# Attention and MLP in one layer: each step's scores from one half of the array's rows, and eight products with v in a row on the other half

## The chip, the cores and the metric

One core of a Trainium2 chip. The metric is the device time of one execution in microseconds; the median of the runs is compared. A profile is one further execution with the hardware profiler, and its times are used for the analysis.

## The reference

```python
xn = layernorm(x)                                   # x: 1 x 2048 x 512, float32
qkv = xn @ wqkv; q, k, v = split in 32 heads of 16
p = softmax(einsum("bhqd,bhkd->bhqk", q, k) * 16 ** -0.5)
A = einsum("bhqk,bhkd->bhqd", p, v).merge_heads() @ wo
B = gelu(xn @ w1 + b1) @ w2 + b2                    # hidden size 1792
out = x + A + B
```

All inputs are float32. The kernel splits the operands of most products into two float16 parts (high and low), and three products of parts stand for one.

## The kernel before

**Tiling.** The 32 heads are eight groups of four; the 2048 queries are four blocks of 512. Group and block give 32 blocks of work, and each has 16 units; a unit is a step of `unit` (512 steps in all). Everything on TensorE (PE) in the main part uses one half of the array's rows (a *side*: rows 0 to 63 or 64 to 127) and a quarter of its columns per instruction; `tiled` (L195) issues four instructions, one per quarter, and this is called a *group of four* or, for short, a product. Two heads lie on each side: heads 0 and 2 on side 0, 1 and 3 on side 1.

**A step** (`unit`, L581) makes, for each of the four heads:

- `s_half` (L238): a score tile with queries as rows into a bank S (three banks), and on VectorE (DVE) the maximum along it (L250). These serve the *later* step: after 16 steps the block's maxima are negated (L261), transposed and turned into two float16 rows (`store`, L264: PE, DVE, GpSimd, then DMAs to `m_d` and from there into two spare rows of the query tile `qst`).
- `e_half` (L286), LEAD = 20 steps behind `s_half`: a score tile with keys as rows into a bank T (three banks); the two spare rows subtract the maximum; ScalarE (ACT) writes the exponential (L297) into a tile `pe`, of which there are 12.
- `v_half` (L300): the float32 products of the four heads' `pe` with v on one side, accumulated over the whole block in one bank V. The array's quarters hold the four heads. A block's sums need both sides of each unit, so V is written by both sides in turn.

A step has two halves. In each the order on PE is: score for the maximum, score for the exponential, twice, alternating between the sides; then `v_half` on one side (r = 1 in the first half, for the unit two steps back, r = 0 in the second, one step back); then `dense` products on the other side.

**Dense work** comes from a generator in `Group`s: the projections of q and k for later heads (24 groups, 12 products a side), then the MLP for four blocks of 512 tokens (14 hidden groups of 12, then 4 groups of 42), then the output projection. How many are issued in a half step is the group's `pace`: FAST four, SLOW three, MEAN three and four in turn (L32). Hidden groups alternate SLOW and FAST (L980), the second matmul is SLOW in the first two blocks and MEAN after (L1000). A group's accumulator is a bank D or T; both sides write it. At its end ACT, DVE (`hh`, L976) or GpSimd work follows.

**Turns.** Two sides must not write one bank at the same time. Before each half step `enter` (L187) sets a goal, and the first v or dense product waits (L173) on one semaphore, `turns`, until the last v and the last dense product of the half before are complete (`leave`, L178). This wait stands in PE's queue, so all that is behind it waits as well.

**Other queues.** The order on every compute engine is the order in which the program issues. GpSimd's work is dosed in `run_steps` (L219) to 2500 ns per step, and things are put off by steps with `later`. All DMAs are issued by SyncE (SP), in order.

**The weight of the output projection**, `wo_s` (L94), is split into two float16 parts in the preparation (L898) and stays in on-chip memory to the end; `wo_l` is a copy of some of its rows on other partitions (L1059). After the MLP its pool is given up, and the pool of the output projection takes the space (L1056).

Of the kernel before, what the change touches and what calls it, by code (L numbers as in the profile page):

```python
# [33 lines left out]
HALF = 1300  # L34
# [13 lines left out]
def layer_kernel(ctx: ExitStack, tc: tile.TileContext, x, wqkv, wo, w1, b1, w2, b2, out):  # L48
# [17 lines left out]
    w2_d = dram.tile([P, 2, NF, D], F16, name="w2_d")  # L66
    acc_d = dram.tile([S, D], F32, name="acc_d")
# [26 lines left out]
    wo_s = const.tile([P, 2, NC, D], F16, name="wo_s")  # L94
# [53 lines left out]
    def split_pool(hi, lo, src, inv):  # L148
        nc.scalar.activation(hi, src, AF.Copy, scale=inv)
        given("act", 1000)  # L150
        nc.gpsimd.tensor_scalar(src, src, inv, 0.0, op0=ALU.mult, op1=ALU.add)
        nc.gpsimd.tensor_tensor(lo, src, hi, op=ALU.subtract)
# [4 lines left out]
    backlog = {"act": 0, "dve": 0}  # L157

    def given(engine, ns):
        backlog[engine] += ns  # L160

    turns = tc.alloc_semaphore("turns")
    counted, left, newest, goal = [0], [], {}, [None]

    def product(user, *args, **kw):

        p = nc.tensor.matmul(*args, **kw)  # L169
        if user is None:  # L170
            return
        if goal[0] is not None:
            p._wait_ge(turns, counted[0])  # L173
            tc.declare_fence(p.ins, group=goal[0])
            goal[0] = None
        newest[user] = p

    def leave(user, goes_on):  # L178

        p = newest.pop(user, None)  # L180
        if p is not None and goes_on:
            p.then_inc(turns, 1)
            tc.no_tile_sem_insts.add(p.ins.name)
            counted[0] += 1
            left.append(p)

    def enter():  # L187

        if left:
            goal[0] = f"turn{counted[0]}"  # L190
            for p in left:
                tc.add_to_no_dep_group(goal[0], p.ins)
            left.clear()

    def tiled(user, dst, lhs, rhs, start, stop):  # L195

        for j in range(0, P, 32):
            product(user, dst[j:j + 32], lhs[:, j:j + 32], rhs, start=start, stop=stop)


    mt_of, ptiles, pv_of = {}, {}, {}
# [36 lines left out]
    def s_half(u, n):  # L238
# [10 lines left out]
        tiled(None, s, qs[p][qb][r, qt * P:(qt + 1) * P], ks[p][kb][r, :], True, True)  # L249
        nc.vector.reduce_max(mt_of[t][:, n, qt, kb:kb + 1], s, axis=AX.X)  # L250
        given("dve", 600)

    def s_end(u):
# [8 lines left out]
        given("dve", 220)  # L262

        def store():  # L264
# [7 lines left out]
            given("dve", 220)  # L272
# [13 lines left out]
    def e_half(u, n):  # L286
# [7 lines left out]
        tiled(None, st, kst[g % 2][p][kt // 4][r, k0:k0 + P], qst[g % 2][p][qb][r, :], True, True)  # L294
        pe = work.tile([P, QB], F32, name="pe", bufs=12)
        ptiles[u, n] = pe
        nc.scalar.activation(pe, st, AF.Exp, scale=sexp[:, g // 2:g // 2 + 1])  # L297
        given("act", 580)

    def v_half(u, a):  # L300

        t, kt = divmod(u, 16)
        g, qb = divmod(t, NQB)
        if kt == 0 and a == 0:
            pv_of[t] = hold("V", "S")
        pv = pv_of[t][0]
        r = slice(64 * a, 64 * a + 64)
        for h in (2, 3, 0, 1):
            c = (4 * g + h) * VW
            product("V", pv[32 * h:32 * h + 32, :], vv[r, kt, c:c + 32], ptiles[u, h][r],  # L310
                    start=(kt == 0 and a == 0), stop=(kt == 15 and a == 1))

    def v_end(u):

        t, kt = divmod(u, 16)
        g, qb = divmod(t, NQB)
        for h in range(4):
            del ptiles[u, h]
        if kt < 15:
            return  # L320
# [3 lines left out]
        given("act", 600)  # L324
# [12 lines left out]
        def inverse():  # L337
            nc.vector.reciprocal(dn, dn)
            given("dve", 330)
# [64 lines left out]
    class Group:  # L404
# [15 lines left out]
        def product(self, side):  # L420
# [11 lines left out]
            tiled("D", self.bank, lhs[r], rhs[r], start, self.last and self.over())  # L432
# [43 lines left out]
    def project(m, w, sb, wh, bank, early=False):  # L476
# [6 lines left out]
        def finish(pj):  # L483
# [5 lines left out]
            given("act", 600)  # L489
# [51 lines left out]
    def ended():  # L541

        if cur[0] is not None and cur[0].over():
            done, cur[0] = cur[0], None
            done.end()
# [10 lines left out]
    def dense(gen, side):  # L556

        f = group(gen)
        for _ in range(0 if f is None else f.pace[pos[0] % 2]):
            if not f.usable(side):  # L560
                return
            f.product(side)

# [9 lines left out]
    def unit(gen):  # L573


        u = pos[0]
        e = u - LEAD
        if u == LEAD and cur[0] is not None:
            burst(gen, cur[0].left())
        pos[0] += 1  # L580
        for a in range(2):  # L581
            for b in range(2 * a, 2 * a + 2):
                if u < NU:
                    s_half(u, b)
                if 0 <= e < NU:
                    e_half(e, b ^ 1)
            if e >= 0:
                enter()

                w, r = (e - 2, 1) if a == 0 else (e - 1, 0)  # L590
                live = 0 <= w < NU
                new = r == 0 and w % 16 == 0
                if live and not new:
                    v_half(w, r)
                dense(gen, 1 - r)
                if live and new:
                    v_half(w, r)

                for user, goes_on in (("V", live and not (r == 1 and w % 16 == 15)),
                                      ("D", cur[0] is not None and not cur[0].over())):  # L600
                    leave(user, goes_on)
# [525 lines left out]
```

## Time and profile before

| | us |
|---|---|
| median of 3 runs | 1575.26 (1571.25 to 1576.23) |
| the profiled execution, device time | 1573.2 |
| its span, first to last instruction | 1571.4 |
| PE busy | 1514.5 |
| DVE busy | 1418.4 |
| ACT busy | 1368.2 |
| GpSimd busy | 668.9 |

The granted TensorE clock is 0.991 of full speed in the mean. A matmul's span in the profile has a modelled end, and neighbours overlap, so busy shares of PE, DVE and ACT run somewhat high; the distance between starts is the better measure. PEld is the loading of weights. A chain of waits is followed back from the last instruction; each piece is the work, or the transfer, that ended last.

### The profile page before, as it was taken

The page shows a single profiled execution, that of the slowest core. Times are in us where ns is not written, and L with a number is a line of the kernel's source. Part 1 is how long each engine was busy: PE and PEld are TensorE (multiplying, and loading weights), DVE is VectorE, ACT ScalarE, POOL GpSimd, SP SyncE. Part 2 cuts the span into 40 slices and gives each one's busy share as a digit, 9 for nine tenths or more (in the row PEclk, how much of TensorE's full clock was granted, in tenths as well). Part 3 has the DMA queues.
Part 4 walks back from the last instruction along what each step waited for, and adds up shares of the span by engine and source line. Part 5 has one row for each costly group of instructions (what it writes and reads, how often), then busy time and mean ns, then how long its engine had stood idle before and what let it go on. Part 6 is the DMA issues. An engine that isn't in the chain of part 4 may idle for free.

```text
span 1571.4 us, 85965 instructions
## 1 busy us (share of the span) xinstructions
PE 1514.5 (96%) x38915; PEld 813.5 (52%) x38915; DVE 1418.4 (90%) x2388; ACT 1368.2 (87%) x2254; POOL 668.9 (43%) x742
## 2 busy tenths in 40 slices
PE   8997998999999999999999999999999999999998
PEld 3433554545555555555455555555555555555443
DVE  7896997989999999999899999999999999999911
ACT  4314998989999999999899999999999999999893
POOL 3113586717774211667511147781116775211000
PEclk9998999999999999999999999999999999999999
DMA  6466366361112111121111111221112110102323
GB/s 205 131 209 219 110 173 209 120 197 48 47 46 67 41 34 38 55 57 45 54 36 51 34 51 44 58 72 33 34 47 59 42 35 15 38 26 86 97 86 102
DMA packets 120248, 123.71 MB, mean 79 GB/s; under 512 B 38988, under 2 KB 90572, under 8 KB 119880
## 3 DMA queue, kind: packets, MB, share of 16 engines
q1 hardware_dynamic: 119880, 118.21, 25.0%
q8 instruction: 304, 4.98, 1.3%
q14 instruction: 64, 0.52, 0.1%
HBM read 80.61 MB, written 37.34 MB: 75 GB/s over the span
## 4 chain that ended last, share of the span: by engine, by line
PE 67%; DVE 20%; DMA 5%; POOL 3%; issue 2%; SPq 1%; ACT 1%; DVEq 0%; POOLq 0%
PE pV L169 20%; DVE mt L250 16%; PE pD L169 15%; PE pS L169 14%; PE pT L169 13%; DVE hh L976 2%; DMA wch<-in_B_w_dram 1%; PE pD L428 1%; DMA m_d<-mhl 1%; PE pT L428 1%; DVE amx L637 1%; SPq L355 1%; PE pT L521 1%; DMA qst<-m_d 1%; PE pS L428 0%
## 5 line engine op out<-in xcount | busy, mean ns | idle before, releaser
L297 ACT ACTIVATE pe<-pT,sexp 128x512 f32<-128x512 f32 x2048 | 1266.7, 689 | 81.3 <-PE pT L169 34.5
L250 DVE TENSOR_REDUCE mt<-pS 128x1 f32<-128x512 f32 x2048 | 1289.2, 683 | 47.5 <-PE pS L169 29.2
L169 PE MATMUL pV<-pe,vv 64*32 64x512 f32 x8192 | 1078.8, 597 | 1.1 <-PE pS L169 0.7
L169 PE MATMUL pT<-qst,kst 64*32 64x512 f16 x8192 | 708.2, 379 | 11.0 <-DMA qst<-m_d 7.8
L169 PE MATMUL pS<-kst,qst 62*32 62x512 f16 x8192 | 637.9, 380 | 30.1 <-DVE mt L250 25.4
L169 PEld LDWEIGHTS <-qst 62*32 62x32 f16 x8192 | 279.8, 92 | 269.0 <-issue 131.1
L169 PEld LDWEIGHTS <-kst 64*32 64x32 f16 x8192 | 295.1, 91 | 183.4 <-issue 68.5
L169 PE MATMUL pD<-xb,wc 64*32 64x512 f16 x5376 | 363.2, 378 | 2.5 <-DMA kst<-qk_d 2.5
L169 PE MATMUL pD<-w_s,g 64*32 64x512 f16 x5376 | 365.4, 377 | 0.0
L169 PEld LDWEIGHTS pV<-pe,vv 64*32 64x32 f32 x8192 | 181.7, 105 | 96.3 <-PE pS L169 7.6
L169 PEld LDWEIGHTS <-wc 64*32 64x32 f16 x5376 | 121.0, 92 | 55.9 <-issue 6.3
L169 PEld LDWEIGHTS <-g 64*32 64x32 f16 x5376 | 112.1, 91 | 44.7 <-issue 0.4
L169 PE MATMUL pD<-xt,wqk_h 64*32 64x512 f16 x1920 | 126.5, 380 | 0.3 <-issue 0.3
L994 POOL TENSOR_TENSOR xa<-xa,yt 128x512 f32<-128x512 f32 x16 | 20.4, 1275 | 236.3 <-ACT yt L992 236.3
L956 POOL TENSOR_TENSOR t<-hh 128x512 f32<-128x512 f32 x56 | 58.1, 1038 | 116.1 <-DVE hh L976 115.0
L348 POOL TENSOR_TENSOR osb<-osb,rb 128x512 f32<-128x512 f32 x31 | 39.8, 1285 | 156.3 <-DMA rb<-den_d 87.7
L274 POOL TENSOR_SCALAR mhl<-msb 64x64 f16<-64x64 f32 x32 | 7.6, 237 | 172.9 <-DVE msb L271 172.9
L958 POOL TENSOR_TENSOR t<-t,hh 128x512 f32<-128x512 f32 x56 | 71.7, 1280 | 4.7
L951 POOL TENSOR_TENSOR t<-t,hh 128x512 f32<-128x512 f32 x56 | 71.6, 1279 | 4.7
L953 POOL TENSOR_TENSOR g<-t,g 128x512 f16<-128x512 f32 x56 | 65.2, 1163 | 4.4
L169 PEld LDWEIGHTS <-wqk_h 64*32 64x32 f16 x1920 | 43.3, 92 | 16.0 <-issue 1.1
L169 PE MATMUL pD<-wo_s,oc 64*32 64x512 f16 x768 | 50.5, 378 | 0.0
(138 smaller groups left out, 869.4 us busy)
## 6 DMA issues: line engine op xcount, KB each, us to landing
wch<-in_B_w_dram SPq DMA_DIRECT2D x28, 512.0 KB
wc<-w_d SPq DMA_DIRECT2D x56, 256.0 KB
qk_d<-stg SPq DMA_DIRECT2D x32, 256.0 KB
rb<-den_d SPq DMA_DIRECT2D x124, 64.0 KB
kst<-qk_d SPq DMA_DIRECT2D x128, 48.0 KB
qst<-qk_d SPq DMA_DIRECT2D x128, 48.0 KB
xs<-in_A_x_dram SPq DMA_DIRECT2D x16, 256.0 KB
qk_d<-stg SPq DMA_DIRECT2D x32, 128.0 KB
```

What stands on the lines that cost most here:

```text
L169: p = nc.tensor.matmul(*args, **kw)
L250: nc.vector.reduce_max(mt_of[t][:, n, qt, kb:kb + 1], s, axis=AX.X)
L297: nc.scalar.activation(pe, st, AF.Exp, scale=sexp[:, g // 2:g // 2 + 1])
L348: pooled((1280, lambda: nc.gpsimd.tensor_tensor(osb, osb, rb, op=ALU.mult)), (620, lambda: nc.gpsimd.tensor_scalar(ot[:, 0], osb, 1.0, 0.0 ...
L355: nc.sync.dma_start(ot_d[64 * g + DH * h:64 * g + DH * h + DH, :, qb * QB:(qb + 1) * QB], ot[32 * h:32 * h + DH])
L428: nc.tensor.matmul(self.bank, lhs, rhs, start=start, stop=self.last and self.over())
L951: (1280, lambda: nc.gpsimd.tensor_tensor(t1, t1, hh, op=ALU.mult)),
L953: (1160, lambda: nc.gpsimd.tensor_tensor(g[:, 1, f, :], t1, g[:, 0, f, :], op=ALU.subtract)),
L956: pooled((1040, lambda: nc.gpsimd.tensor_tensor(t1, hh, hh, op=ALU.mult)), (620, lambda: nc.gpsimd.tensor_scalar(t1, t1, 1.0, 1.0 / GELU_A ...
L958: (1280, lambda: nc.gpsimd.tensor_tensor(t1, t1, hh, op=ALU.mult)),
L976: nc.vector.tensor_scalar(hh, hp, scale, bias, op0=ALU.mult, op1=ALU.add)
L994: add = lambda: nc.gpsimd.tensor_tensor(xa, xa, yt, op=ALU.add)
```

## The change

- **One side per step for the scores.** With r the parity of the step, a step makes the score tiles of the two heads on side r for two units (its own and its neighbour), instead of those of all four heads for one unit. Over two steps the same tiles are made.
- **v on the other side.** `v_turn` issues in a step all products with v that are due on side 1 - r: those of tiles made at least two steps before, which is eight, two groups of four heads. A tile is thus read by one side two steps after it is made and by the other side three steps after.
- **Order in a step:** some dense products on side 1 - r (pace less two), the first scores, two more dense on side 1 - r, the second scores, four products with v, the third scores, four products with v, the fourth scores, dense products on side r. A dense group may end, and the next begin, at any product.
- **Turns apart.** v and dense products have a semaphore each, and a product waits only where its own kind changes sides.
- **Exponential tiles:** 17 fixed buffers instead of a pool of 12. Every eighth exponential names the exponential four before it as a dependency.
- **wo** is split like the other weights into a buffer and stored in DRAM (`wo_d`); after the MLP it is loaded into the output projection's pool.
- Counters without effect (`given`, `backlog`) go.

```diff
-    turns = tc.alloc_semaphore("turns")
...
+    turns = {user: tc.alloc_semaphore(f"turns{user}") for user in "VD"}
+    counted, newest = dict.fromkeys(turns, 0), {}
+    def product(user, side, *args, **kw):
         p = nc.tensor.matmul(*args, **kw)
         if user is None:
             return
+        before = newest.get(user)
+        if before is not None and before[0] != side:
+            counted[user] += 1
+            before[1].then_inc(turns[user], 1)
...
+            p._wait_ge(turns[user], counted[user])
+            tc.declare_fence(p.ins, group=group)
+        newest[user] = side, p
...
-        pe = work.tile([P, QB], F32, name="pe", bufs=12)
+        pe = pes[used[0] % len(pes)]
+        used[0] += 1
         ptiles[u, n] = pe
-        nc.scalar.activation(pe, st, AF.Exp, scale=sexp[:, g // 2:g // 2 + 1])
+        for side in due:
+            side.append((pos[0], u, n))
+        ex = nc.scalar.activation(pe, st, AF.Exp, scale=sexp[:, g // 2:g // 2 + 1])
+        exps.append(ex.ins.name)
+        if len(exps) % 8 == 1 and len(exps) > 8:
+            tc.add_manual_dep(ex.ins, exps[-5], AFTER, reason="buffers")
+
+    def v_turn(a, step):
+        todo = {h: [w for w in due[a] if w[0] <= step and w[2] == h] for h in (a, 2 + a, 1 - a, 3 - a)}
+        due[a][:] = [w for w in due[a] if w[0] > step]
+        while any(todo.values()):
+            for h in todo:
+                if todo[h]:
+                    v_one(a, *todo[h].pop(0)[1:])
+            yield
...
+        r = e % 2
+        v = v_turn(1 - r, pos[0] - (2 if e < NU else 0))
+        def scores(i):
+            k, n = divmod(i, 2)
+            if u - r < NU:
+                s_half(u - r + k, 2 * n + r)
+            if e - r < NU:
+                e_half(e - r + k, 2 * n + r)
+        pace = cur[0].pace if cur[0] is not None else FAST
+        dense(gen, 1 - r, pace[0] - 2)
+        scores(0)
+        dense(gen, 1 - r, 2)
+        scores(1)
+        next(v, None)
+        scores(2)
+        next(v, None)
+        scores(3)
+        for _ in v:
+            pass
+        dense(gen, r, pace[1])
+        for t in [t for t in pv_of if summed[t] == [32] * 4]:
+            v_end(t)
...
+        wo_s = p3.tile([P, 2, NC, D], F16, name="wo_s")
         wo_l = p3.tile([64, 2, D], F16, name="wo_l")
-        nc.sync.dma_start(wo_l, wo_s[64:128, :, NC - 1, :])
+        nc.sync.dma_start(wo_s, wo_d)
+        nc.sync.dma_start(wo_l, wo_d[64:128, :, NC - 1, :])
```

More of the change, by code (lines that the diff above doesn't have):

```diff
@@ L66, in layer_kernel @@
     w2_d = dram.tile([P, 2, NF, D], F16, name="w2_d")
+    wo_d = dram.tile([P, 2, NC, D], F16, name="wo_d")
     acc_d = dram.tile([S, D], F32, name="acc_d")
@@ L93, in layer_kernel @@
     nc.gpsimd.memset(vv[:, :, H * VW:], 0.0)
-    wo_s = const.tile([P, 2, NC, D], F16, name="wo_s")
     sexp = const.tile([P, 4], F32, name="sexp")
@@ L431, in product @@
             self.at[side] += 1
-            tiled("D", self.bank, lhs[r], rhs[r], start, self.last and self.over())
+            tiled("D", side, self.bank, lhs[r], rhs[r], start, self.last and self.over())
         def over(self):
@@ L544, in ended @@
             done, cur[0] = cur[0], None
+            newest.pop("D", None)
             done.end()
@@ L554, in burst, with dense @@
             ended()
[L556 to L561, printed above, removed]
+    def dense(gen, side, n):
+        while n > 0 and (f := group(gen)) is not None and f.usable(side):
             f.product(side)
+            n -= 1
+            ended()
     def land():
@@ L577, in unit @@
         e = u - LEAD
-        if u == LEAD and cur[0] is not None:
-            burst(gen, cur[0].left())
-        pos[0] += 1
[L581 to L601, printed above, removed]
-                for k in backlog:
-                    backlog[k] = max(0, backlog[k] - HALF)
-                if live and r == 1:
-                    v_end(w)
-                ended()
-        if u < NU:
+        if e < 0:
+            pos[0] += 1
+            for n in range(4):
+                s_half(u, n)
+            s_end(u)
+            burst(gen, LFILL[u - 16])
+            tick()
+            return
+        if e == 0 and cur[0] is not None:
+            burst(gen, cur[0].left())
+        r = e % 2
[20 more added lines that the diff above has]
+            v_end(t)
+        for key in [k for k in ptiles if not any(w[1:] == k for side in due for w in side)]:
+            del ptiles[key]
+        pos[0] += 1
+        if u < NU and r:
             s_end(u)
-        if u < LEAD:
-            burst(gen, LFILL[u - 16])
         tick()
```

87 lines of the change are left out of this document (25 added, 62 removed).

## The prediction

> **What bounds the kernel now.** I read the page first (parts 1 and 4), then busy time by stage, then the instructions of one step in order of time, then the chain of waits.
>
> ```profile
> span 1571.4 us, 85965 instructions
> ...
> PE 1514.5 (96%) x38915; PEld 813.5 (52%) x38915; DVE 1418.4 (90%) x2388; ACT 1368.2 (87%) x2254; POOL 668.9 (43%) x742
> ...
> PE 67%; DVE 20%; DMA 5%; POOL 3%; issue 2%; SPq 1%; ACT 1%; DVEq 0%; POOLq 0%
> ```
>
> Three engines are nearly full, so the question is which one paces a step, and whether the others could follow if it went faster. A step makes four score tiles for the maximum (DVE), four for the exponential (ACT), eight products with v, and six to eight dense groups. The reductions of a stage, divided by four, count its steps:
>
> ```profile
> 510.00:630.00 120.00, 119.82 (x3336) 68.32 (x3328) 117.31 (x195) 116.05 (x192) 19.52 (x22) 1.00 0.13 38
> ...
> L250 DVE TENSOR_REDUCE mt<-pS 128x1 f32<-128x512 f32 x185 | 116.6, 683 | 2.0 <-PE pS L169 0.9 <-PE pT L169 0.5
> ...
> L250 DVE TENSOR_REDUCE mt<-pS 128x1 f32<-128x512 f32 x130 | 83.1, 684 | 1.9 <-PE pS L169 0.6 <-PE pT L169 0.4
> ...
> L250 DVE TENSOR_REDUCE mt<-pS 128x1 f32<-128x512 f32 x129 | 80.3, 681 | 1.9 <-PE pS L169 0.9 <-PE pT L169 0.6
> ...
> L976 DVE TENSOR_SCALAR hh<-pD,fac,b_s 128x512 f32<-128x512 f32 x9 | 7.3, 810 | 0.2
> ...
> L250 DVE TENSOR_REDUCE mt<-pS 128x1 f32<-128x512 f32 x252 | 160.1, 684 | 7.7 <-PE pS L169 3.2 <-PE pT L169 0.7
> ```
>
> The first row is a stage with its length and the busy time of PE, PEld, DVE, ACT and POOL. The others are groups in the windows 510 to 630 (second matmul, pace 3), 1333 to 1418 (second matmul, pace 3 and 4), 377 to 466 (hidden layer, pace 3 and 4 in turn) and 141 to 326 (projections, pace 4). Steps: 185/4 = 46.25 in 120 us is **2.595 us**; 130/4 in 85 is **2.615**; 129/4 in 89 is **2.76**; 252/4 in 185 is **2.94**, with stalls.
>
> Now one half step at pace 3, in order of time (start, duration):
>
> ```profile
> 801.02 0.62 PE L169 MATMUL pV<-pe,vv 64*32 64x512 f32 x4
> ...
> 801.05 0.61 PE L169 MATMUL pD<-w_s,g 64*32 64x512 f16 x8
> ...
> 801.46 0.61 PE L169 MATMUL pV<-pe,vv 64*32 64x512 f32 x4
> ...
> 801.49 0.39 PE L169 MATMUL pD<-w_s,g 64*32 64x512 f16 x4
> ...
> 801.71 0.39 PE L169 MATMUL pT<-qst,kst 64*32 64x512 f16 x4
> ...
> 801.89 0.42 PE L169 MATMUL pS<-kst,qst 62*32 62x512 f16 x8
> ...
> 802.11 0.40 PE L169 MATMUL pT<-qst,kst 64*32 64x512 f16 x4
> ...
> 802.28 0.13 PEld L169 LDWEIGHTS pV<-pe,vv 64*32 64x32 f32 x5
> 802.29 0.63 PE L169 MATMUL pV<-pe,vv 64*32 64x512 f32 x4
> ```
>
> Three things are to be seen. First the unit: dense groups of one side start 0.22 us apart (801.05, two of them, then 801.49, then the score at 801.71); a float32 group of four heads makes two passes 0.44 apart, 0.88 us, four units. Second, the order: pT at 801.71 starts before pS at 801.89, although `s_half` is issued before `e_half`, and dense products start between the two passes of the v group that stands ahead of them. **The two sides of the array run past each other.** Third, the wait: the second pass of v ends at 801.46 + 0.61 = 802.07, and only 0.21 us later do the weights of the next v group load. That is the turn: v on the other rows may start only when v on these rows is complete. The chain 0.44 + 0.61 + 0.21 = 1.26 us per half step, 2.52 per step, is what paces pace 3; PE's work is less: each side has 22 units in two steps (8 scores, 8 of v, 6 dense), 11 x 0.22 = 2.42. At pace 3 and 4 it is 11.5 units, 2.53, at pace 4 it is 12, 2.64.
>
> What the others could do:
>
> ```profile
> 535.35 2.54 DVE mt L250 x4
> ...
> 540.70 2.40 DVE mt L250 x4
> ...
> 755.39 0.81 DVE hh L976
> ```
>
> In the chain of waits four reductions take 2.54 in the ordinary step and 2.40 where DVE has fallen behind (after the maximum of a block). So DVE's floor is 2.40; the small operations of a block add, as my estimate, 0.05 per step (some 0.8 us in 16 steps), 2.45; in the hidden layer one `hh` of 0.81 comes every 3.5 steps, 0.23 more, 2.68. ACT:
>
> ```profile
> 342.42 2.47 ACT pe L297 x4
> ```
>
> four exponentials in the chain, 2.47: ACT could follow to about there, and 2.47 is an upper bound of its floor, since neighbours overlap and the last one counts whole.
>
> **The change, part by part.** *Turns.* Before, v and dense share one semaphore and every half step starts with a wait for both. After, v has its own and changes rows once per step, dense too, at another place in the step. v's chain per step: first group 0.88, then 0.44 + 0.61 + 0.21, together 2.14 us, against 2.52 before: it falls below PE's own work, so the wait is gone from the path. Dense: its last product on one side (before the second scores) and its first on the other (after the fourth) are four scores on the side it goes to, 0.88, apart, against 0.39 + 0.21 for completion and semaphore: covered by 0.28; and with that cover gone it would cost that difference each step.
>
> *What is late next.* PE's 2.42 and DVE's 2.45 at pace 3. Both can be had only if scores are early enough for DVE. The scores of a step now come in a row on one side, two units apart, then nothing comes until the next step. There are three banks, each handed back about every 0.60. From handing back to the end of the next reduction in it: 0.40 (pS above) + 0.68 (mean reduction) + some 0.1 of semaphores = 1.18, and three banks at 0.60 are 1.80: a score may start 0.6 us late before DVE idles. Walking one side: v ends, four scores and four exponentials' tiles follow (the third and fourth held by their banks), then the six dense, then v again: 22 units in a period of 2 x 2.45 = 22.3, so the first score stands some 0.4 us behind its bank. Less than 0.6: it fits, barely. I take 2.48 for pace 3 (floor 2.45, little rub), 2.56 for pace 3 and 4 (PE 2.53), 2.69 in the hidden layer (DVE 2.68). At pace 4 PE has its 2.64 as before: nothing.
>
> *By stages.* Steps: a hidden group has 12 products a side, 4 steps at pace 3 and 3 at pace 4, 14 groups are 49, four blocks 196. A group of the second matmul has 42: 14 steps at pace 3, two blocks of four, 112; 12 steps at pace 3 and 4, 96. Projections about 72, the output projection the other 36, and of those the last 20 have no maximum. Gains: 112 x (2.595 - 2.48) = 13; 96 x (2.615 - 2.56) = 5; 196 x (2.76 - 2.69) = 14; projections 0. For the last:
>
> ```profile
> 1504.00:1545.00 41.00, 40.59 (x1000) 17.21 (x992) 3.25 (x5) 39.92 (x66) 3.07 (x3) 1.00 0.29 90
> ...
> L297 ACT ACTIVATE pe<-pT,sexp 128x512 f32<-128x512 f32 x65 | 40.3, 687 | 1.1
> ```
>
> DVE is idle there (3.25), 65 exponentials in 41 us are 2.52 a step, again v's turn, and ACT's 2.47 is next: 20 x 0.05 = 1, more if ACT's floor lies lower; the 16 before them like pace 3, 2. Together **35 us**.
>
> *What stays.* Whole-kernel stalls that hang on transfers do not care for the order of the products:
>
> ```profile
> 250.56 5.22 DMA dn<-den_d
> ...
> 326.50 5.14 DMA kst<-qk_d
> ...
> 763.81 6.61 DMA m_d<-mhl
> ...
> 1448.84 6.17 DMA oc<-ot_d
> 1455.02 4.82 DMA m_d<-mhl
> ```
>
> The rows that carry the block's maximum have four steps from reduction to first use; a faster step leaves them 0.1 x 4 = 0.4 us less, which only the few late blocks feel: 0 to 3 us, I take 1.
>
> *Buffers and wo.* 17 exponential tiles instead of 12: v now reads a tile two and three steps after it is made, 16 tiles and one; without the five more ACT would wait for v each step. The tile wo_s leaves for a dram copy: two stores of 0.5 MB among the 28 like them, and a load of 1 MB ahead of the output projection, on SP's queue ahead of the spread of the sums and of the oc tiles; PE's first product with it blocks all behind it. The load stands before a row that shows 6.17 for a like burst of transfers: from 0 (the queue has room there, v and scores run on) to 6 us; I take 2. *Banks.* At a block's end two v banks are held for part of a step (two left for S), and a dense group that starts right behind another takes a bank whose exponential is one newer than the score's: bounds 0 and one exponential spacing, 0.6 us, for 32 blocks and 108 groups, 0 to 84; the nearest rows show DVE-paced steps where PE has that slack, so I take 2. Below nothing none of these goes, as none removes work. Sum: 35 - 1 - 2 - 2 = 30 from the profiled execution's 1573.2 is 1543. A unit of 0.22 is rounded up: the v group at 801.02 lets pS start on its rows at 801.89, 0.87 for four units, 0.2175, 1% of 2.53 to 2.64 in the 168 steps where PE paces, 4 us: **1539**. The median of the runs, 1575.3, is 2 us above the profiled one, which I leave as it is; 0.3%, about 5 us, is what a measurement here tells from no change.
>
> **The rivals.** *Strict order on PE (slower).* If no product could start before the one ahead of it, the new order is worse than the old: one side does its last two score tiles (2 units), all dense (pace sum, 6 to 8) and a v group (4) before the other side's second v group may go: 12, 13 and 14 units per step, against 11, 11.5 and 12. Prices: 96 x (2.86 - 2.615) = 24; hidden, (4 x 12 + 3 x 14)/7 = 12.9 units, 2.83, 196 x 0.07 = 14; projections 72 x (3.08 - 2.64) = 32 at most; pace 3 112 x 0.045 = 5; about **1645**. It decides from the point where a product has more than some groups to pass. Against it stands the row at 801.71. For it: the rows show a product passing two dense groups or one score tile, no more, and a wait still holds what stands behind it. A milder form (passing, but not far enough) lies between, 1580 to 1600. Together 0.18.
>
> The Trainium skill, page "TensorE: Matmul & The Clock Gate", section "Part 3: Packing small matmuls — row/col tiling", states exactly this order: weight loads are pulled ahead, but matmuls start and end strictly in program order. This case's trace does not agree: pT at 801.71 starts ahead of pS at 801.89, which the program issues first. By the page the time would be that of this rival; by the row, the forecast.
>
> *DVE keeps what PE gives (less gain).* The hidden layer stays at 2.76, because DVE's `hh` and the bursts of scores collide, and late transfers eat the rest: 13 + 5 + 3 less 5, **1557**, between 1555 and 1570; 0.15. *No change* (1570 to 1580): the same with bank waits of the upper kind, 0.07. *More gain*: every stage at its floor and the waits at block ends gone, 35 + 112 x 0.06 + 96 x 0.08 + 20 x 0.1 + 72 x 0.2 is some 66, **1507**; for it, the projections' 2.94 is well above 2.64; 0.12. The forecast, 1515 to 1555, has 0.48.
>
> **How the numbers follow.** Faster: 0.48 + 0.15 + 0.12 = 0.75; same 0.07; slower 0.18. The range runs from 1502, beyond the large gain, to 1590, inside the mild slower case; above it about 0.12 is left out, below 0.05.
>
> **What would show it.** In the profile after: v groups of one side start 0.88 apart, and first groups one step, 2.5, apart; the gap between v's last pass and the other side's v weights well over 0.21; in 120 us of pace 3 some 193 (480/2.48) reductions instead of 185, and DVE's four in the chain at 2.40; the hidden layer at 2.69. Wrong would be: PE waiting on pS for DVE in most steps with DVE idle too (banks), v pairs starting late behind dense groups of the same step (order), or a stall of over 5 us at the first product with wo_s.

## The result and the profile after

| | before | after |
|---|---|---|
| median, us | 1573.26 (1570.34 to 1576.23, 4 runs) | **1634.35** (1630.98 to 1636.07, 4 runs) |
| ratio | | 1.0386, 95% interval 1.0357 to 1.0415 |
| span of the profiled execution | 1571.4 | 1629.1 |

The change costs 61 us; the prediction said a gain of 34. The page of the changed kernel, parts 1, 4 and 5 (total and mean of a group, then the idle time of its engine ahead of it and what ended most of it):

```profile
span 1629.1 us, 85743 instructions
...
PE 1583.1 (97%) x38915; PEld 965.3 (59%) x38915; DVE 1425.7 (88%) x2388; ACT 1383.9 (85%) x2254; POOL 668.5 (41%) x742
...
PE 84%; DVE 5%; DMA 4%; POOL 3%; SPq 1%; issue 1%; ACT 1%; POOLq 0%; DVEq 0%; ACTq 0%
...
L283 ACT ACTIVATE pe<-pT,sexp 128x512 f32<-128x512 f32 x2048 | 1284.3, 688 | 124.3 <-PE pT L161 87.6
L236 DVE TENSOR_REDUCE mt<-pS 128x1 f32<-128x512 f32 x2048 | 1299.7, 683 | 99.1 <-PE pT L161 70.8
...
L161 PE MATMUL pS<-kst,qst 62*32 62x512 f16 x8192 | 856.1, 381 | 16.5 <-DVE mt L236 15.3
```

DVE and ACT do the same work and wait more: DVE is idle for 99.1 us ahead of its maxima (the idle time that stands first behind the second bar). The same row of the page before:

```profile
L250 DVE TENSOR_REDUCE mt<-pS 128x1 f32<-128x512 f32 x2048 | 1289.2, 683 | 47.5 <-PE pS L169 29.2
```

From 47.5 to 99.1 are 51.6 us; the span grew by 57.7. The maxima wait for PE; PE stands idle ahead of a score, waiting for DVE, for 15.3 us only. The chain's DVE share fell from 20% to 5%, so it is not DVE's own work that got longer. By stage, in windows as long as those of the prediction (120, 85, 89 and 185 us: second matmul at pace 3, at pace 3 and 4, hidden layer, projections), the groups of the changed kernel:

```profile
L236 DVE TENSOR_REDUCE mt<-pS 128x1 f32<-128x512 f32 x183 | 114.5, 682 | 4.9 <-PE pT L161 3.3 <-PE pD L161 0.4
...
L236 DVE TENSOR_REDUCE mt<-pS 128x1 f32<-128x512 f32 x125 | 79.6, 684 | 5.3 <-PE pT L161 4.1
...
L236 DVE TENSOR_REDUCE mt<-pS 128x1 f32<-128x512 f32 x125 | 79.0, 683 | 4.3 <-PE pT L161 3.4 <-PE pD L161 0.2
...
L236 DVE TENSOR_REDUCE mt<-pS 128x1 f32<-128x512 f32 x240 | 155.9, 685 | 17.9 <-PE pT L161 12.9 <-PE pS L161 2.6 <-PE pD L161 0.2
```

| stage | reductions before, after | step before, after | steps | difference, us |
|---|---|---|---|---|
| second matmul, pace 3 | 185, 183 | 2.595, 2.623 | 112 | +3 |
| second matmul, pace 3 and 4 | 130, 125 | 2.615, 2.720 | 96 | +10 |
| hidden layer | 129, 125 | 2.76, 2.848 | 196 | +17 |
| projections | 252, 240 | 2.94, 3.083 | 72 | +11 |

That is 41 of the 57.7. A count is good to about one reduction, which is 1 to 5 us in a row of the table. The last 48 steps and wo are in none of the four. One stall adds 7.5: the longest step after the projections is 15.49 us between exponentials, where before had 7.95.

**One step, walked.** PE, then DVE, then ACT of the changed kernel at pace 3 in order of time (start, duration; in brackets the idle time ahead and what ended it):

```profile
830.26 0.61 PE L161 MATMUL pV<-pe,vv 64*32 64x512 f32 x4
...
831.82 0.63 PE L161 MATMUL pV<-pe,vv 64*32 64x512 f32 x4
...
832.26 0.61 PE L161 MATMUL pV<-pe,vv 64*32 64x512 f32 x4
...
832.65 0.40 PE L161 MATMUL pS<-kst,qst 62*32 62x512 f16 x4
832.69 0.61 PE L161 MATMUL pV<-pe,vv 64*32 64x512 f32 x4
832.87 0.40 PE L161 MATMUL pT<-qst,kst 64*32 64x512 f16 x4
...
833.12 0.61 PE L161 MATMUL pV<-pe,vv 64*32 64x512 f32 x4
```

```profile
831.77 1.89 DVE L236 TENSOR_REDUCE mt<-pS 128x1 f32<-128x512 f32 x3
833.85 3.25 DVE L236 TENSOR_REDUCE mt<-pS 128x1 f32<-128x512 f32 x5 [0.19 <-PE pT L161]
```

```profile
833.91 3.25 ACT L283 ACTIVATE pe<-pT,sexp 128x512 f32<-128x512 f32 x5 [0.20 <-PE pT L161]
```

The step's fourth score starts at 832.65 and ends at 833.05. DVE is free from 831.77 + 1.89 = 833.66, and yet the reduction starts only at 833.85. What ended in between is v: its last pass, 833.12 + 0.61 = 833.73, belongs to a group that the program issues *ahead* of this score, on the other rows. The score itself ran past that group. ACT shows the same: the fourth tile pT ends at 833.27, its exponential starts at 833.91. The profile names pT as the releaser of a maximum that reads pS; as I read it, several reports came at once, and the last of them is named.

The step is no exception. Between 797.5 and 924 us, 20 of the 48 fourth maxima of a step find DVE idle for 0.1 us or more, and one of the 143 others. Between 137 and 1440 us, 284 maxima do, with 77 us of idle time; 228 of them, with 44 us, start 0.10 to 0.15 us after the end of a v pass. In the kernel before it is one of 98.

### The profile page after: what moved, and what is told of

Same layout as the page of the kernel before. It is cut to its first block, busy times and chain, and to the rows that moved or that the text cites. A ratio compares the mean times of both kernels' runs of the same rounds, so it can differ in the third digit from the quotient of the medians.

```text
span 1629.1 us, 85743 instructions
## 1 busy us (share of the span) xinstructions
PE 1583.1 (97%) x38915; PEld 965.3 (59%) x38915; DVE 1425.7 (88%) x2388; ACT 1383.9 (85%) x2254; POOL 668.5 (41%) x742
## 4 chain that ended last, share of the span: by engine, by line
PE 84%; DVE 5%; DMA 4%; POOL 3%; SPq 1%; issue 1%; ACT 1%; POOLq 0%; DVEq 0%; ACTq 0%
PE pV L161 29%; PE pD L161 26%; PE pS L161 13%; PE pT L161 11%; DVE mt L236 3%; PE pD L418 1%; DMA wch<-in_B_w_dram 1%; PE pT L418 1%; SPq L345 1%; DVE amx L634 1%; PE pT L510 1%; DMA wc<-w_d 0%; POOL osb L338 0%; DMA m_d<-mhl 0%; DMA qst<-m_d 0%
## 5 line engine op out<-in xcount | busy, mean ns | idle before, releaser
L283 ACT ACTIVATE pe<-pT,sexp 128x512 f32<-128x512 f32 x2048 | 1284.3, 688 | 124.3 <-PE pT L161 87.6
L236 DVE TENSOR_REDUCE mt<-pS 128x1 f32<-128x512 f32 x2048 | 1299.7, 683 | 99.1 <-PE pT L161 70.8
L161 PE MATMUL pV<-pe,vv 64*32 64x512 f32 x8192 | 989.6, 591 | 1.2 <-issue 1.2
L161 PE MATMUL pS<-kst,qst 62*32 62x512 f16 x8192 | 856.1, 381 | 16.5 <-DVE mt L236 15.3
L161 PE MATMUL pT<-qst,kst 64*32 64x512 f16 x8192 | 857.3, 379 | 5.6 <-DMA qst<-m_d 3.8
L161 PEld LDWEIGHTS <-qst 62*32 62x32 f16 x8192 | 326.7, 90 | 205.5 <-issue 146.9
L161 PE MATMUL pD<-xb,wc 64*32 64x512 f16 x5376 | 333.0, 377 | 11.4 <-DMA wc<-w_d 11.4
L161 PE MATMUL pD<-w_s,g 64*32 64x512 f16 x5376 | 331.5, 375 | 0.0
L161 PEld LDWEIGHTS pV<-pe,vv 64*32 64x32 f32 x8192 | 276.1, 107 | 89.2 <-issue 39.7
L161 PEld LDWEIGHTS <-wc 64*32 64x32 f16 x5376 | 160.4, 92 | 92.0 <-issue 13.4
L161 PEld LDWEIGHTS <-g 64*32 64x32 f16 x5376 | 162.5, 92 | 72.0
```

The source lines that it names most:

```text
L283: ex = nc.scalar.activation(pe, st, AF.Exp, scale=sexp[:, g // 2:g // 2 + 1])
```

## The experiments

A *report* is the signal by which an engine that waits learns that a product is complete. **Theory A**: products pass one another between the two halves of the rows, but PE reports them complete in program order. A score behind v on the other side is reported when v is complete, its reduction is late, its bank comes back late, and the next score waits. **Theory B**: the products themselves start late, v above all. **Theory C**: the loss lies elsewhere (transfers, wo). Where a later run has other rivals, its expectation names them.

**v one place later.** In `unit`:

```diff
         scores(1)
-        next(v, None)
         scores(2)
         next(v, None)
         scores(3)
```

> The changed kernel with each group of four v products issued one pair of scores later (after the third and after the fourth). Theory A (products start side by side, but PE reports completion in program order, so DVE and ACT hear of a score behind v only when v is complete): the third score is no longer held and the fourth only by a group that is nearly done; pace 3 goes from 2.62 to 2.48-2.55 us per step, the total to 1560-1600 us. Theory B (the rival on record: products also start in program order): v and with it the other side's next scores come two units, 0.43 us, later in each step; the total rises to 1700-1830. Theory C (the loss sits at the wo transfers and the block ends): no change, 1634 within 5.

Measured: **1584.22** (1582.26 to 1593.99), ratio to the kernel before 1.009 (1.0062 to 1.0118). Taking out one line takes off 50 of the 61 us by the medians, 46 by the ratios. The same four stages in its trace, and DVE and ACT at pace 3:

```profile
L236 DVE TENSOR_REDUCE mt<-pS 128x1 f32<-128x512 f32 x186 | 114.6, 680 | 4.1 <-PE pT L161 1.7 <-PE pS L161 1.7
...
L236 DVE TENSOR_REDUCE mt<-pS 128x1 f32<-128x512 f32 x132 | 81.9, 682 | 2.9 <-PE pT L161 1.3 <-PE pS L161 0.6
...
L236 DVE TENSOR_REDUCE mt<-pS 128x1 f32<-128x512 f32 x129 | 79.5, 679 | 3.2 <-PE pT L161 2.0 <-PE pS L161 1.0
...
L236 DVE TENSOR_REDUCE mt<-pS 128x1 f32<-128x512 f32 x247 | 153.5, 681 | 16.8 <-PE pT L161 9.5 <-PE pS L161 6.7
```

```profile
839.53 6.78 DVE L236 TENSOR_REDUCE mt<-pS 128x1 f32<-128x512 f32 x11
```

```profile
839.73 6.74 ACT L283 ACTIVATE pe<-pT,sexp 128x512 f32<-128x512 f32 x11
```

Eleven reductions and eleven exponentials in a row without a gap, 6.78/11 x 4 = 2.47 a step at most: with one score fewer held behind v, DVE and ACT run through in such stretches. The stage as a whole doesn't reach that: 186 reductions in 120 us are 2.58 a step, against 2.62 in the changed kernel and the 2.48 to 2.55 that A expected here. A has the total right and the step wrong. The holds behind v are gone: of the 150 maxima between 137 and 1440 us that find DVE idle for 0.1 us or more, none starts 0.10 to 0.15 us after a v pass. The second matmul is a little ahead of the kernel before (186 and 132 reductions against 185 and 130).

**v one place earlier.**

```diff
         dense(gen, 1 - r, 2)
-        scores(1)
         next(v, None)
-        scores(2)
+        scores(1)
         next(v, None)
+        scores(2)
         scores(3)
```

> The changed kernel with each group of four v products issued one pair of scores earlier (after the first and after the second). Theory A: the second score is held as well, and the third and fourth for longer; DVE and ACT idle 0.2-0.4 us more in each step; total 1720-1840 us. Theory B: v may go two units earlier in each step, where its side is free; total 1570-1630. Theory C: no change, 1634 within 5.

Measured: **1776.0**, ratio 1.129 (1.1236 to 1.1345). From its page:

```profile
span 1773.5 us, 85744 instructions
...
L236 DVE TENSOR_REDUCE mt<-pS 128x1 f32<-128x512 f32 x2048 | 1321.6, 684 | 224.4 <-PE pT L161 199.2
```

One score more behind v, and DVE's wait goes from 99.1 to 224.4 us. B, by which an earlier v should help, falls.

**The kernel before, with only the wo part.** `wo_s` in a DRAM copy and loaded after the MLP, as in the change; all else as before.

```diff
-    wo_s = const.tile([P, 2, NC, D], F16, name="wo_s")
+    wo_d = dram.tile([P, 2, NC, D], F16, name="wo_d")
...
+        wo_s = p3.tile([P, 2, NC, D], F16, name="wo_s")
+        nc.sync.dma_start(wo_s, wo_d)
```

> The kernel before with only the part of the change that stores wo in DRAM and loads it after the MLP. Theories A and B: nearly nothing, 1573-1580 us. Theory C: a good part of the 61 us, 1590 or more.

Measured: 1577.28, ratio 1.0032 (1.0013 to 1.0051): 5 us by the ratio, between 2 and 8. C is not the cause; the prediction had 2 of a range from 0 to 6. Its trace shows what costs:

```profile
295.96 0.56 SPq L898 DMA_DIRECT2D wo_d<-wsp  x1
...
302.81 0.34 DVE L338 RECIPROCAL dn<-dn 64x32 f32<-64x32 f32 x1 [2.58 <-DMA dn<-den_d]
```

A store of wo stands on SP ahead of a block's sums, and DVE, in order, waits 2.58 us for them, where the kernel before does not wait. From 306 us on its exponentials are 2 to 5 us behind those of the kernel before, and 4.6 at the last one: in this trace the stores of the preparation cost, and the load after the MLP adds nothing.

**Reports measured by themselves.** A small kernel that computes no layer: a score on one half of the rows, its reduction, and on the other half a v group (b) or six dense groups ahead of it (c) or behind it (d).

> No layer at all (the output is zeros): a score tile on side 1 and its reduction on DVE, six times each, (a) ahead of a v group on side 0, (b) behind a v group on side 0, (c) behind six dense products on side 0, (d) ahead of six dense products, (e) behind two v groups, (f) behind a v group on its own side. Theory A: in a and d the reduction starts 0.1-0.2 us after the score's end; in b, c and e the score starts at once too, but its reduction starts 0.1-0.2 us after the end of the v group or of the sixth dense product, about 0.6, 1.2 and 1.5 us after the score's own end. Theory B: in b, c and e the score itself starts late, no earlier than the last product ahead of it, and its reduction follows its own end at once. If neither holds, b, c and e look like a.

Measured, one execution of b and one of d in order of time (PE, ACT and DVE; `other` is v in b and dense in d, and ACT reads it when it is complete):

```profile
47.92 1.05 PE L79 MATMUL other_b<-pe,vv 64*32 64x512 f32 x6 [1.43 <-ACT pe L90]
48.39 0.39 PE L71 MATMUL score_b<-wide,narrow 64*32 64x512 f16 x2
...
48.40 0.59 PE L79 MATMUL other_b<-pe,vv 64*32 64x512 f32 x1
49.11 0.60 ACT L89 ACTIVATE osb<-other_b 128x512 f32<-128x512 f32 x1 [1.24 <-PE other_b L79]
49.12 0.69 DVE L74 TENSOR_REDUCE mx<-score_b 128x1 f32<-128x512 f32 x1 [0.78 <-PE other_b L79]
```

```profile
115.48 0.40 PE L71 MATMUL score_d<-wide,narrow 64*32 64x512 f16 x4 [1.88 <-DVE wide L91]
115.49 2.01 PE L85 MATMUL other_d<-wide,narrow 64*32 64x512 f16 x24
115.92 0.69 DVE L74 TENSOR_REDUCE mx<-score_d 128x1 f32<-128x512 f32 x1 [0.50 <-PE score_d L71]
```

In b the score starts when its operand is ready (DVE writes `wide` until 48.34), beside v's second passes, and by the profile's modelled ends it ends 0.2 us before them (48.78 against 48.99), but its reduction starts at 49.12, together with the reader of v. In d the same score is issued first: its reduction starts 0.04 us after its end at 115.88, although dense runs on to 117.50. All six repetitions of each show it, behind v 0.118 to 0.128 us after v's end, behind dense 0.100 to 0.111 after the sixth group's end, ahead of dense 0.047 to 0.052 after the score's own end. Behind two v groups (e) it is 0.117 to 0.128 after the second's end, on v's own rows (f) some 0.04 after the score's. Case a, the score ahead of v, shows 0.052 in its first repetition alone: in the others the first v product was issued ahead of the score, and the reduction comes 0.26 to 0.91 us late. d is the clean case, and c against d is the test: in both, dense runs beside the score, and only the order of issue differs.

**Dense later as well as v.** v one place later, and the other side's dense products one score later:

```diff
-        dense(gen, 1 - r, pace[0] - 2)
         scores(0)
-        dense(gen, 1 - r, 2)
+        dense(gen, 1 - r, pace[0] - 2)
         scores(1)
-        next(v, None)
+        dense(gen, 1 - r, 2)
         scores(2)
```

> The changed kernel with v's products one place later (as in the run with v later) and the other side's dense products one score later as well: first score; dense; second score; dense; third score; v; fourth score; rest of v. Theory A (a product is reported complete only when all that the program issues ahead of it are complete, so a score behind the other side's products hands its bank to the reduction late): the first score of a step now has no product of its own step ahead of it, so at pace 4 it is no longer held by dense; pace-4 steps fall from 2.8 to about 2.7, the hidden layer from 2.78 to about 2.70 (DVE's floor 2.68), together 15 to 35 us below the 1584 of v later: 1550 to 1570. Theory B (only the place of v matters, dense groups are too short to hold a score): within 8 us of v later, 1576 to 1592. Theory C (dense products that stand behind a score which waits for a bank are late themselves and make v late): slower than v later, 1595 or more.

Measured: 1582.56 (1579.72 to 1587.23), ratio 1.0057 (1.0036 to 1.0078). By the medians this is within 2 us of v later alone, by the ratios 5 below, with intervals that overlap: my extension of A to dense products missed. The traces say how. With v later alone, 127 of its 150 maxima that find DVE idle start 0.065 to 0.115 us after the end of a dense product; here 47 of 142 do, and 122 start 0.03 to 0.07 us after the end of their own score. Their idle time is 66 and 58 us. So the holds behind dense groups went, and the scores came late instead: those holds are not what the hidden layer and the projections pay for once v is out of the way.

**Only dense later**, v where the change has it.

```diff
-        dense(gen, 1 - r, pace[0] - 2)
         scores(0)
-        dense(gen, 1 - r, 2)
+        dense(gen, 1 - r, pace[0] - 2)
         scores(1)
+        dense(gen, 1 - r, 2)
         next(v, None)
```

> The changed kernel with only the dense products of the other side one score later; v stays where the change put it. Theory A: one hold of two goes at pace 4 (the first score's), v's hold of the third and fourth scores stays: 10 to 30 us below the changed kernel's 1634, and still above 1595; pace 3 stays at 2.53 to 2.60. Theory B (dense does not hold scores): 1628 to 1642. Theory C (dense behind waiting scores is late): 1645 or more.

Measured: **1663.89** (1661.35 to 1664.85), ratio 1.0569 (1.0545 to 1.0594): some 29 us *slower* than the changed kernel where I had expected a gain. Its window of 120 us at pace 3:

```profile
L236 DVE TENSOR_REDUCE mt<-pS 128x1 f32<-128x512 f32 x177 | 111.1, 683 | 9.0 <-PE pT L161 6.1 <-PE pD L161 0.2
```

177 reductions against 183, and DVE's idle time 9.0 against 4.9. The two dense groups now stand between the second score and v on v's own rows, so v starts and ends later, and the third and fourth scores behind it are held longer. The trace shows the longer holds: between 137 and 1440 us, 421 maxima with 94 us of idle time start 0.10 to 0.15 us after a v pass, against 228 with 44 us. That the two dense groups are what delays v is how I read it; no run took this apart.

**Half the maximum, in both kernels.** `reduce_max` over 256 of the 512 columns; half of the keys are left out of the maximum.

```diff
-        nc.vector.reduce_max(mt_of[t][:, n, qt, kb:kb + 1], s, axis=AX.X)
+        nc.vector.reduce_max(mt_of[t][:, n, qt, kb:kb + 1], s[:, :QB // 2], axis=AX.X)
```

> The kernel before with the maximum taken over 256 of the 512 columns of each score tile (half of the keys are left out of the maximum): DVE's work per step falls from about 2.4 to about 1.6 us. Theory A (at pace 3 v's chain of turns, 1.26 per half step, paces the kernel before): the step at pace 3 stays at 2.50 to 2.58 (2.59 before), the hidden layer falls to 2.55 to 2.68 since there DVE's share is the largest; in all 1515 to 1560. Theory B (DVE paces pace 3 of the kernel before as well): pace 3 falls to 2.40 to 2.48, in all below 1515.

> The changed kernel with the maximum taken over 256 of the 512 columns of each score tile (half of the keys are left out of the maximum). Theory A (the turn wait is gone, and what the changed kernel loses is the wait of scores for banks that come back late): a reduction that is 0.3 us shorter gives each bank back 0.3 earlier, which is most of the wait of about 0.36 per cycle of two steps: pace 3 falls to 2.44 to 2.54 and the whole by 40 to 90 us, to 1545 to 1595; if it stops at the upper end, the exponentials' banks, which are held in the same way and are not changed here, are the next. Theory B (products of the changed kernel wait for one another on PE itself, and banks do not matter): pace 3 stays at 2.54 to 2.60 and the whole above 1610.

Measured: the kernel before **1555.38**, ratio 0.9884 (0.9861 to 0.9907); the changed kernel **1587.89**, ratio 1.0084 (1.0057 to 1.0112). First the kernel before, then the changed one, 120 us at pace 3:

```profile
L250 DVE TENSOR_REDUCE mt<-pS 128x1 f32<-128x256 f32 x186 | 70.3, 419 | 44.5 <-PE pS L169 24.2 <-PE pT L169 20.2
```

```profile
L283 ACT ACTIVATE pe<-pT,sexp 128x512 f32<-128x512 f32 x187 | 114.1, 693 | 4.4 <-PE pT L161 2.1 <-PE pS L161 0.3 <-PE pS L252 0.2
...
L236 DVE TENSOR_REDUCE mt<-pS 128x1 f32<-128x256 f32 x186 | 75.0, 421 | 42.9 <-PE pT L161 25.2 <-PE pS L161 14.8 <-PE pS L252 1.4
```

In the kernel before, taking 46 us of work from DVE in that window (116.6 to 70.3) gives one reduction more (186 against 185): DVE does not pace its pace 3, as the prediction said of the turns. In the changed kernel the same cut gives 46 us in all, against 19 in the kernel before: there the reduction's length counts, as it must if it is part of the way by which a late bank comes back. The step stops at 2.58 (120 x 4/186), just above my bound of 2.54, with ACT busy for 114 of 120 us; the exponentials' banks, held in the same way, were left as they are.

**Idle calls ahead of the hidden layer.** The generator of the MLP first yields eight times nothing, so that the weights can land. A call of `dense` uses up one, and the changed step has three calls where the step before had two. Counted in the traces, the last projection stands at step 60.0 in both, the first hidden product at 65.5 before and 64.0 after.

```diff
-        for _ in range(8):
+        for _ in range(12):
             yield None
```

> The changed kernel with 12 instead of 8 idle calls ahead of the hidden layer. Both kernels finish the last projection at step 60.0; the first hidden product stands behind 65.5 steps of exponentials' scores in the kernel before and behind 64.0 in the changed one, because each call of dense uses up one idle yield and the changed step calls dense three times instead of two (8/3 steps against 8/2). Twelve restore four steps. Theory A (PE waits at the head of the hidden layer for the weights' transfer, whose landing does not depend on PE): the step of 15.5 us there shrinks by the 1.33 steps that run meanwhile, to about 12, and the whole by about 3 us, 1628 to 1633. Theory B (the transfers wait for PE's progress and move along): the step stays at 15 or more and the time at 1634 or above.

Measured: 1627.61 (1626.18 to 1628.96), ratio 1.0349 (1.0328 to 1.0369); the long step is 11.49 us instead of 15.49, the profiled span 4.3 us shorter, the median 6.7. PE's wait there, in the changed kernel and then in this run:

```profile
343.58 1.04 PE L161 MATMUL pD<-xb,wc 64*32 64x512 f16 x8 [11.40 <-DMA wc<-w_d]
```

```profile
343.54 0.61 PE L161 MATMUL pD<-xb,wc 64*32 64x512 f16 x4 [8.48 <-DMA kst<-qk_d]
```

The wait ends at the same time, 343.5, though the profile names another transfer of the same burst the second time; PE only reaches it later. The landing is set by the queue of transfers: in the chain of the changed kernel, the stores of the last block's result stand ahead of the weights.

```profile
328.43 1.18 POOL ot L340
...
329.63 0.55 SPq L345
...
335.12 0.66 SPq L925
...
335.82 7.76 DMA wc<-w_d
```

SP issues that store (L345) when GpSimd has made it, and the weights (L925) 5.5 us behind it; the kernel before, by the row at 326.50 in the prediction, was through with its transfer at 331.64.

The same line with v one place later (18 and 12 calls), and 12 calls in the kernel before:

> v one place later, with 18 idle calls (6 steps) ahead of the hidden layer. Theory A (as for 12 calls): 3.3 more steps run while the weights land, the stall of 15.5 us falls to about 7, the whole from 1584 by 6 to 10 us to 1573 to 1578, within 0.4% of the kernel before. Theory B (transfers move along, or the products displaced to later steps cost what is saved): 1581 or above.

> The kernel before with 12 idle calls, 6 steps instead of 4, so that the run before can be judged by the same measure. Its stall at that place is a step of 7.95 us; theory A: two more steps run meanwhile, the stall goes to 2.6 to 4 us and the whole falls by 3 to 5 us, to 1567 to 1572. Theory B: no change, within 2 us of the kernel before.

> v one place later and the idle calls restored to four steps (12): the two mended together. If the terms add up (v's place 50 us, idle calls 4 us by the profiled execution of the run with 12 calls, wo 5 us left in), the time is 1584 less 4: 1577 to 1582, 4 to 9 us above the kernel before, which is what wo costs. If the displaced dense products come back as a stall in the output projection (as with 18 calls), it stays at 1583 or above.

Measured: 1583.64, ratio 1.007 (1.0053 to 1.0087); 1579.61, ratio 1.0037 (1.002 to 1.0053); 1586.39, ratio 1.0082 (1.0066 to 1.0099). None gains; the kernel before loses some 6 us. With 18 calls the dense products that were put off are missing at the other end, where PE waits anew in the output projection:

```profile
1450.45 0.62 PE L161 MATMUL pD<-wo_s,oc 64*32 64x512 f16 x4 [4.54 <-DMA oc<-ot_d]
```

The long step with 12 calls and v later is 11.6 instead of 15.5 us, as in the changed kernel, but the last 48 steps take 4 us more. So the terms do not add up as I had set down, and the fewer idle calls are worth some 4 us in the changed kernel and nothing net with v later.

**Is it counting?** In the run of reports every product raised the one counter that the reduction waits on, so order could come from counting. In the last run v (g) and dense (h) raise no counter until the end; only the scores do. In i, v follows the score on the same rows.

> Products and reductions alone, no layer is computed and the output is zeros. A v group (case g) or six dense groups (case h) on one half of the rows, a score on the other half behind them, its reduction; eight times. In the run of signals every product raised the one counter on which the reduction waits, so the order seen there could come from counting. Here v and dense raise no counter until the eighth time (their bank is read once, at the end): the count that the reduction waits for is reached by the score's own signal. Theory A (PE gives its signals in program order): the reductions of the first seven times start 0.10 to 0.15 us after the end of the v group (g) or the last dense group (h) ahead, where these end after the score. Theory C (only the counting holds them): they start 0.04 to 0.06 after the score's own end in all of these.

Measured, a repetition each of g, h and i (in g the row at 15.81 is the reduction of the score before):

```profile
15.70 0.40 PE L71 MATMUL score_g<-wide,narrow 64*32 64x512 f16 x4
15.81 0.69 DVE L74 TENSOR_REDUCE mx<-score_g 128x1 f32<-128x512 f32 x1 [0.17 <-PE score_g L71]
15.96 1.04 PE L79 MATMUL other_g<-pe,vv 64*32 64x512 f32 x8
...
16.67 0.69 DVE L74 TENSOR_REDUCE mx<-score_g 128x1 f32<-128x512 f32 x1 [0.17 <-PE score_g L71]
...
32.32 0.40 PE L71 MATMUL score_h<-wide,narrow 64*32 64x512 f16 x4
32.52 1.46 PE L85 MATMUL other_h<-wide,narrow 64*32 64x512 f16 x24
33.42 0.69 DVE L74 TENSOR_REDUCE mx<-score_h 128x1 f32<-128x512 f32 x1 [0.60 <-PE score_h L71]
...
55.02 0.59 PE L71 MATMUL score_i<-wide,narrow 64*32 64x512 f16 x4
55.23 1.23 PE L79 MATMUL other_i<-pe,vv 64*32 64x512 f32 x8
55.45 0.69 DVE L74 TENSOR_REDUCE mx<-score_i 128x1 f32<-128x512 f32 x1 [0.38 <-PE score_i L71]
```

The score that starts at 15.70 ends at some 16.09; its reduction starts at 16.67, 0.10 us after the v group ahead of it ends (16.57; the row at 15.96 holds that group's second pass and the next group's first). In the first seven repetitions each, all reductions start 0.100 to 0.101 us after v's end, and 0.085 to 0.086 after the end of the sixth dense group; with nothing ahead that ends later (i), they start 0.046 to 0.051 after the score's own end. The count is not what holds them: **PE gives its reports in program order.** The changed kernel agrees: by its program, only the last of its 4096 v products (8192 passes in the profile) raises the counter on which the reductions wait. As a matmul's end is modelled in the profile, the runs do not tell whether a held product is complete and unreported, or itself ends late; for its reader this is the same.

## Why the prediction was wrong

*What bounds the kernel before.* Right as far as tried: with DVE's work cut by half, its pace 3 stayed at 2.58. That it is the turns and not ACT, busy for 116 of the 120 us in the prediction's first row of stages, no run took apart.

*"The two sides run past each other."* Right for starts. From this I priced only starts. **The step that failed** is the walk of a bank: "From handing back to the end of the next reduction in it: 0.40 (pS above) + 0.68 (mean reduction) + some 0.1 of semaphores = 1.18". In the changed kernel the fourth score starts at 832.65 and its reduction at 833.85: 1.20, where the walk had 0.40 + 0.1, and with 0.68 it is 1.88. Between 797.5 and 924 us 1.20 is also the median of the fourth scores. Three banks at 0.60 give 1.80. The prediction's "0.6 us late before DVE idles" was in truth a small deficit for such a score, and the new order puts two of a step's four score pairs behind a float32 group that reports 0.44 + 0.61 us after its start.

*Turns.* Right: the v groups of one side start 0.87 apart (831.82, 832.69), and v's last pass on the other rows ends at 830.26 + 0.61 = 830.87, 0.95 us ahead of the first of them, against 0.21 before: this wait has left the path. What that should have released came only in part. With v one place later some stretches run at 2.47, but pace 3 as a whole stays at 2.58, where 2.48 was forecast; and from step 66, the head of the hidden layer, to step 470, the end of the MLP, that kernel gains 5 us on the kernel before (the same exponential starts 11.0, then 6.0 us behind), of the 32 forecast there. So the reports explain most of the loss. Why most of the gain stays away without it, they don't explain.

*Stages.* Forecast 13, 5, 14 and 0 us of gain; measured +3, +10, +17 and +11 of loss.

*The strict-order rival*, 1645 at 0.18 with its milder form, lies nearer, but with another mechanism: as far as the traces go, products are not held, their reports are. The Trainium skill, page "TensorE: Matmul & The Clock Gate", section "Part 3: Packing small matmuls — row/col tiling", has matmuls start and end strictly in program order. Of the ends, as reported, this case's runs agree (0.10 us after v's end, thirteen repetitions behind v and no exception); of the starts they don't (the fourth score starts at 832.65, the v group issued ahead of it at 832.69). I had seen the half that is not so and dropped the whole rule.

*What stays.* wo was put at 2 us and is 5 (2 to 8), paid, by the trace above, for the stores and not for the load. The head of the hidden layer was not in the sum at all: three calls instead of two use up the idle calls sooner, 4 us, and the store that stands ahead of the weights makes it longer.

*Open.* With v later, 9 us of span remain above the kernel before; wo is some 5, the longer stall ahead of the hidden layer 7.5 before what the stages give back. Why pace 3 stays at 2.58 there, why the projections stay near 3.0 at PE's 2.64, what two banks for v at a block's end cost, and whether dense turns are covered as I put it, no run took apart. No version of the change beats the kernel before.

## What to carry to other kernels

Where short and long products run side by side on the row halves of TensorE, as here, price a short product by the time at which the longest one issued ahead of it ends, not by its own end; only then walk its bank. Issue the products whose readers set the pace ahead of the long ones, even where the long ones could start at once. And where a step is cut into more calls, look for counters that count calls.

## What the runs showed of the hardware

- Between the row halves a later product starts, and by its modelled end also ends, ahead of an earlier one, but in the two small kernels its reduction starts 0.085 to 0.128 us after the end of everything issued ahead, against 0.038 to 0.052 after its own end where nothing that ends later stood ahead.
- The profile's releaser can then be a product that is not read: `other_b` for a reduction of `score_b`, and pT for 70.8 of the 99.1 us that maxima of pS wait.
